# Filling a tile of partial maxima half a head early, and an eighth PSUM bank for the run-ahead maxima

## Chip, core and metric

One core of one Trainium2 chip. The metric is the device time of one execution in microseconds, the median over several runs. The engines named below are PE (TensorE, with PEld for its weight loads), DVE (VectorE), ACT (ScalarE), POOL (GpSimd) and SP (SyncE, which issues most of the DMAs). Each engine works through its own queue in order, and waits on semaphores for the others.

## What is computed

Two full multi-head attentions over the same input, mixed by a gate of each token. x has 2048 tokens of 512 features; each attention (A and B) has 32 heads of 16 features, and all is float32.

```python
def mha(x, wqkv, wo):                      # once with A's weights, once with B's
    q, k, v = split((x @ wqkv))            # 32 heads, 16 features each
    scores = einsum("bhqd,bhkd->bhqk", q, k) * 16 ** -0.5
    o = einsum("bhqk,bhkd->bhqd", softmax(scores, axis=-1), v)
    return o.reshape(1, 2048, 512) @ wo

g = sigmoid((x * gate_w).sum(-1, keepdims=True))
return g * mha(x, wqkv_a, wo_a) + (1 - g) * mha(x, wqkv_b, wo_b)
```

## The kernel before

The order of all instructions on every engine is written by hand (a manual schedule); only the semaphores come from the framework, which also rotates the buffers of each tile name. So an instruction can wait for another engine, but never moves past one ahead of it in its own queue.

**Prologue.** x and the weights are split into a high part and a low rest, and q, k and v are projected from these (`project_qk`, L237; `project_v`, L262) into PSUM tiles `ps_pro` (two tiles of two banks each). The results go to DRAM and come back in a stacked layout, `q_st` and `k_st` (three buffers each, one for each head in flight).

**Maxima ahead of the scores.** The softmax needs the maximum of each row of scores. The kernel computes the scores twice: once only for the maxima, some 20 tiles of 128 queries ahead of their use, and once for the exponentials. A tile of maxima has 2048 keys in four parts of 512. `max_part` makes one part: a PE matmul into one bank of `ps_m` (L124, three banks) and a DVE reduction (L130) to one column of `mxp[h]`, a tile of 128 x 16 x 4 for a head h. `max_excess` and `max_pair` make two parts at once, by an ACT step (L139) and a fused DVE step (L146). As a pair then leaves one of the four columns of `mxp` unwritten, the tile is filled with a very low number first (L118, on POOL). `mxp` rotates over two buffers. In `max_tile` the fill is issued when the first part of a head's first tile is, directly ahead of it in program order. When a head is complete, `max_split` reduces the four columns to one (L154, DVE), and POOL splits the result into two parts (`mparts`, L155 and L156); `max_rows` transposes them (L161, DVE) and sends them through DRAM into rows of `q_st`, from where the score matmuls subtract them.

**Run-ahead.** The first 80 parts (20 tiles) are made in the prologue: `run_ahead(n)` pops n parts, from the tenth block of `project_qk` on and between the tiles of the second attention's `project_v`, four after nearly every tile. In the prologue `ps_m` holds three banks and `ps_pro` four; one of the eight is not used. After the prologue `ps_pro`'s banks go to `ps_st` (four banks of scores) and the eighth to `acc`.

**Main loop.** 64 heads of 16 rounds; one iteration is two rounds, r and r+1, so a head has eight iterations. The order within an iteration is a string,

```python
FULL = "mree2emem3ememef3me"
```

in which e is a block of scores with its exponential (`score`: PE L614 into `ps_st`, ACT L616), m, r and f are `max_part`, `max_excess` and `max_pair` for the tile 20 rounds ahead, and a digit is that many quarters of the product of the probabilities with V (`attend_next`, PE L565, accumulated in `acc`, evicted once a head by ACT, L582). At the first digit the output projections that are due (`project_out`, L449, with their DVE steps L453 or L455) are put in, and, one iteration after the end of a head of maxima, `max_rows`. The variable m is r + 20, so the maxima are one head and four rounds ahead. Side work is due at fixed rounds through `later` and is issued at the start of an iteration: gate products (POOL, L346, L353), loads of V (POOL's queue, L177), loads of the output weights (L388 to L390), reciprocals of the denominators (L404), normalising (POOL, L422) and splitting (POOL, L427, L428). In the last iteration of a head of maxima `max_split` is issued at its end; the next iteration begins with the side work that is due, and then `max_part` of the new head, with the fill.

Of the kernel before, what the change touches and what calls it, by code (L numbers as in the profile page):

```python
# [23 lines left out]
F32 = mybir.dt.float32  # L24
# [5 lines left out]
PSUM = bass.MemoryType.PSUM  # L30
DRAM = bass.MemoryType.DRAM

P = 128
# [4 lines left out]
NT = S // P  # L38
KC = DM // P
NQ = S // 512  # L40
NG = DM // P
HG = H // NG
NH = 2 * H
# [3 lines left out]
LOWEST = -3.0e38  # L47
# [6 lines left out]
def gated_mha(ctx: ExitStack, tc: tile.TileContext, xT, x, wqkv_a, wo_a, wqkv_b, wo_b, gate_w, out):  # L54
    nc = tc.nc
    pe, act, dve, pool = nc.tensor, nc.scalar, nc.vector, nc.gpsimd
# [6 lines left out]
    ps_m = ctx.enter_context(tc.tile_pool(name="ps_m", bufs=3, space=PSUM))  # L63
# [23 lines left out]
    def load_stacks(h, halves=HALVES):  # L87
        dma = nc.sync.dma_start
        s, hh = divmod(h, H)
        g, j = divmod(hh, HG)  # L90
        q, k = q_st[h % 3], k_st[h % 3]
        qs, ks = qd[s][g], kd[s][g]

        def pairs(t, step, n):
            v = t[0, j]
            return bass.AP(tensor=v.tensor, offset=v.offset, ap=[[n, DH], [step, 2], [1, n]])

        for b in halves:
            dma(k[b:b + 32].bitcast(F32), pairs(ks, HG * DH * KS, KS))
            dma(q[b:b + 32].bitcast(F32), pairs(qs, 0, S))  # L100
            dma(k[b + 32:b + 48].bitcast(F32), ks[0, j])
            dma(q[b + 32:b + 48].bitcast(F32), qs[1, j])
# [3 lines left out]
    mxp = {}  # L106
# [3 lines left out]
        turn[0] ^= 1  # L110
        return HALVES[1 - turn[0]]

    def max_tile(m):
        h, t = divmod(m, NT)
        if t == 0 and h not in mxp:
            mxp[h] = small.tile([P, NT, NQ], F32, name="mxp")
            if h:
                pool.memset(mxp[h], LOWEST)  # L118
        return h, t

    def max_scores(ps, h, t, c):
        q, k = q_st[h % 3], k_st[h % 3]
        b = rows()
        pe.matmul(ps, q[b:b + SC, t * P:(t + 1) * P], k[b:b + SC, c * 512:(c + 1) * 512], start=True, stop=True)  # L124

    def max_part(m, part):
        h, t = max_tile(m)
        ps = ps_m.tile([P, 512], F32, name="ps_m")
        max_scores(ps, h, t, part)
        dve.tensor_reduce(mxp[h][:, t, part:part + 1], ps, op=ALU.max, axis=AX.X)  # L130

    excess = {}

    def max_excess(m):
        h, t = max_tile(m)
        ps = ps_st.tile([P, 512], F32, name="ps_st")
        max_scores(ps, h, t, NQ)
        excess[m] = work.tile([P, 512], F32, name="excess")
        act.activation(excess[m], ps, AF.Relu)  # L139

    def max_pair(m):
        h, t = divmod(m, NT)
        ps = ps_m.tile([P, 512], F32, name="ps_m")
        max_scores(ps, h, t, 1)
        e = excess.pop(m)
        dve.tensor_tensor_reduce(e, ps, e, 1.0, LOWEST, ALU.add, ALU.max, mxp[h][:, t, 1:2])  # L146
# [3 lines left out]
    def max_split(h):  # L150
        halves = mxp.pop(h)
        m = small.tile([P, NT], F32, name="mrow")
        mp = small.tile([P, 2, NT], F32R, name="mparts")
        dve.tensor_reduce(m, halves, op=ALU.max, axis=AX.X)  # L154
        pool.tensor_copy(mp[:, 0], m)  # L155
        pool.tensor_tensor(mp[:, 1], m, mp[:, 0].bitcast(F32), op=ALU.subtract)  # L156
        mparts[h] = mp

    def max_rows(h):
        mt = small.tile([P, 32], F32, name="mt")  # L160
        dve.transpose(mt, mparts.pop(h).rearrange("p i t -> p (i t)").bitcast(F32))  # L161
        q = q_st[h % 3]
        r = md[h % 3]
        nc.sync.dma_start(r.rearrange("i (t a x) -> a (i t) x", a=4, x=32), mt)
        for b in HALVES:
            nc.sync.dma_start(q[b + SC:b + SC + 2].bitcast(F32), r)
# [11 lines left out]
                       vd[s][c * 512:(c + 1) * 512, o].rearrange("(k p) f -> p k f", p=P))  # L178

    with tc.tile_pool(name="xs", bufs=1) as xs, tc.tile_pool(name="pro", bufs=2) as pro, \  # L180
            tc.tile_pool(name="ps_pro", bufs=2, space=PSUM) as ps_pro:
        xh = [xs.tile([P, KC, 512], F32R, name=f"xh{c}") for c in range(NQ)]
        xl = [xs.tile([P, KC, 512], F32R, name=f"xl{c}") for c in range(NQ)]
        wblocks = {}
# [100 lines left out]
        def run_ahead(n):  # L285
            turn[0] = 0
            for _ in range(n):
                m, part = ahead.pop(0)
                max_part(m, part)
                if (m, part) == (NT - 1, NQ - 1):  # L290
                    max_split(0)
                    pending.append(0)

        pending = []
        for i, (s, g, isk) in enumerate(blocks):
            block(split_w, i + 1)
            block(load_w, i + 3)
            if i in (2, 8):
                load_w(i // 8, 2 * DM, DM)
            if i in (4, 9):  # L300
                split_w(i // 8, 2 * DM, DM)
            project_qk(s, g, isk, lambda: run_ahead((i >= 10) + 2 * (i >= 13)))
            if i in (5, 6, 8, 9):
                load_stacks(i // 8, HALVES[(i - 5) % 3:][:1])
            if i == 7:
                for t in range(NT):
                    project_v(0, t)
            if i == 9:
                for c in range(4):
                    load_v(0, c)  # L310
# [129 lines left out]
    def project_out(side, t):  # L440
        groups = SIDES[side]
        ps = result_bank()
        c, tt = divmod(t, 4)
        sl = slice(tt * P, (tt + 1) * P)
        for G in groups:
            n, g = gh[G] * DH, G % NG
            slot = c if G == LAST else g
            for i, (a, b) in enumerate(((0, 0), (1, 0), (0, 1))):
                pe.matmul(ps, ot[a][:n, slot, sl], wt[b][:n, g], start=G == groups[0] and i == 0,  # L449
                          stop=G == groups[-1] and i == 2)  # L450
        g = gate[min(side, 1)][:, t:t + 1]
        if side == 0:
            dve.tensor_scalar(o_acc[:, t], ps, g, None, op0=ALU.mult)  # L453
        else:
            dve.scalar_tensor_tensor(o_acc[:, t], ps, g, o_acc[:, t], op0=ALU.mult, op1=ALU.add)  # L455
# [132 lines left out]
    def attend_next(n):  # L588
        while n:
            r, qa = divmod(done[0], 4)  # L590
            qb = min(4, qa + n)
            attend(r, qa, qb)
            done[0] += qb - qa
            n -= qb - qa
# [11 lines left out]
    def score(r, c):  # L606
        h, kt = divmod(r, NT)
        if c == 0:
            pt[r] = ppool.tile([P, S], F32, name="p")
        q, k = q_st[h % 3], k_st[h % 3]  # L610
        kk, cc = (4 * (kt % 4) + c, kt // 4) if h == NH - 1 else (kt, c)
        b = rows()
        ps = score_bank(r)
        pe.matmul(ps, k[b:b + SC + 2, kk * P:(kk + 1) * P], q[b:b + SC + 2, cc * 512:(cc + 1) * 512],  # L614
                  start=True, stop=True)
        act.activation(pt[r][:, c * 512:(c + 1) * 512], ps, AF.Exp, scale=SCALE)  # L616
# [7 lines left out]
    for r in range(0, ROUNDS, 2):  # L624
        h, kt = divmod(r, NT)
        projects = []
        for rr in (r, r + 1):
            for fn, a in later.pop(rr, ()):
                if fn is project_out:
                    projects.append(a)  # L630
                else:
                    fn(*a)
        if kt == 0 and h + 2 < NH:
            load_stacks(h + 2)
        m = r + NT + LEAD
        scored, parts = 0, 2
        for step in FULL if m < ROUNDS else ():
            if step == "e":
                score(r + scored // 4, scored % 4)
                scored += 1  # L640
            elif step == "r":
                max_excess(m)
            elif step == "f":
                max_pair(m)
            elif step == "m":
                max_part(m + parts // NQ, parts % NQ)
                parts += 1
            else:
                for a in projects:
                    project_out(*a)  # L650
                projects = []
                turn[0] = 0
                if r:
                    attend_next(int(step))
                if scored > 1 and r in after:
                    max_rows(after.pop(r))
        m += 1
        if m > ROUNDS:
            for rr in (r, r + 1):
                for c in range(4):  # L660
                    score(rr, c)
                attend_next(4 * rr - done[0])
                if r in after:
                    max_rows(after.pop(r))
        if m < ROUNDS and m % NT == NT - 1:
            max_split(m // NT)
            after[r + 2] = m // NT
# [29 lines left out]
```

## Time and profile before

| | |
|---|---|
| time, median of 3 runs | 2902.99 us (2901.59 to 2903.16) |
| the profiled execution's own time | 2899.51 us |
| its span, first to last instruction | 2897.7 us |
| busy share of the span | PE 98%, ACT 84%, DVE 83%, POOL 10% |
| mean granted TensorE clock | 0.992 of full speed |
| fills of the tile of maxima (L118) | 63, some 0.15 us each |

In the lines of the profile shown below, a row of the timeline has its start and duration in microseconds, then engine, line, operation, output <- input, the shapes and a count; in brackets stands the idle time of the engine before it and whose event ended it. A row of the waits has the waiting engine, tile and line, what released it, the total, the number and the longest. A row of a window has its bounds, its length, the busy time of PE, PEld, DVE, ACT and POOL with the number of instructions, the granted clock, the busy share of the DMA engines and GB/s. A row of the chain by line gives the share of the span that the chain which ended last spent there. A wait for several semaphores is put down to the one that came last by the profile.

### The profile page before, as it was taken

The page shows a single profiled execution, that of the slowest core. Times are in us where ns is not written, and L with a number is a line of the kernel's source. Part 1 is how long each engine was busy: PE and PEld are TensorE (multiplying, and loading weights), DVE is VectorE, ACT ScalarE, POOL GpSimd, SP SyncE. Part 2 cuts the span into 40 slices and gives each one's busy share as a digit, 9 for nine tenths or more (in the row PEclk, how much of TensorE's full clock was granted, in tenths as well). Part 3 has the DMA queues.
Part 4 walks back from the last instruction along what each step waited for, and adds up shares of the span by engine and source line. Part 5 has one row for each costly group of instructions (what it writes and reads, how often), then busy time and mean ns, then how long its engine had stood idle before and what let it go on. Part 6 is the DMA issues. An engine that isn't in the chain of part 4 may idle for free.

```text
span 2897.7 us, 65030 instructions
## 1 busy us (share of the span) xinstructions
PE 2851.4 (98%) x26016; PEld 1437.6 (50%) x26016; DVE 2396.4 (83%) x4395; ACT 2420.3 (84%) x4755; POOL 280.0 (10%) x472
## 2 busy tenths in 40 slices
PE   8999999999999999999999999999999999999999
PEld 7876444444444444444444455544444444445554
DVE  3135788999999999999899878899999999988784
ACT  3221689999999999999999868899999999988785
POOL 2120133000000000000100132000000000011201
PEclk9999999999999999999999999999999999999999
DMA  7683334333322333333422433322333343324212
GB/s 260 195 255 122 79 70 92 63 60 60 70 53 51 52 66 67 59 61 59 82 53 53 109 79 83 56 55 51 64 58 60 60 78 70 59 60 98 64 22 90
DMA packets 86085, 231.61 MB, mean 80 GB/s; under 512 B 22134, under 2 KB 32342, under 8 KB 73238
## 3 DMA queue, kind: packets, MB, share of 16 engines
q1 hardware_dynamic: 83222, 218.53, 34.2%
q0 software_dynamic: 2560, 8.91, 1.2%
q8 instruction: 205, 3.36, 0.5%
q14 instruction: 98, 0.80, 0.1%
HBM read 158.46 MB, written 68.94 MB: 78 GB/s over the span
## 4 chain that ended last, share of the span: by engine, by line
PE 83%; DVE 11%; DMA 2%; POOL 2%; issue 1%; SPq 1%; ACT 0%; POOLq 0%; ACTq 0%; DVEq 0%
PE acc L565 33%; PE ps_st L614 26%; PE ps_m L124 13%; DVE mxp L130 8%; PE ps_pro L237 5%; PE ps_pro L262 3%; PE ps_m L449 2%; DVE excess L146 1%; PE ps_st L124 1%; DMA raw<-in_xT 0%; DMA qd<-part 0%; DVE mrow L154 0%; POOL o_num L422 0%; POOL mparts L155 0%; POOL mparts L156 0%
## 5 line engine op out<-in xcount | busy, mean ns | idle before, releaser
L616 ACT ACTIVATE p<-ps_st 128x512 f32<-128x512 f32 x4061 | 2135.1, 628 | 205.1 <-PE ps_m L124 92.9
L130 DVE TENSOR_REDUCE mxp<-ps_m 128x1 f32<-128x512 f32 x3092 | 1984.6, 684 | 251.6 <-PE ps_m L124 97.6
L614 PE MATMUL ps_st<-q_st,k_st 50*128 50x512 f32 x4061 | 1377.5, 442 | 0.3 <-ACT excess L139 0.3
L124 PE MATMUL ps_m<-k_st,q_st 48*128 48x512 f32 x3594 | 1304.2, 448 | 30.1 <-DVE mxp L130 24.5
L565 PE MATMUL acc<-p,vg 128*17 128x256 f32 (+2 forms) x16208 | 1195.4, 388 | 2.6 <-DVE ev L573 1.6
L614 PEld LDWEIGHTS ps_st<-q_st,k_st 50*128 50x128 f32 x4061 | 677.2, 185 | 380.9 <-ACT p L616 219.8
L124 PEld LDWEIGHTS ps_m<-k_st,q_st 48*128 48x128 f32 x3594 | 611.7, 185 | 441.4 <-DVE mxp L130 402.0
L565 PEld LDWEIGHTS acc<-p,vg 128*17 128x17 f32 x16208 | 323.6, 96 | 536.8 <-issue 412.8
L146 DVE CUSTOM_DVE_ANT_0 excess<-ps_m,excess 128x512 f32<-128x512 f32 x502 | 341.7, 681 | 0.0
L139 ACT ACTIVATE excess<-ps_st 128x512 f32<-128x512 f32 x502 | 300.9, 599 | 1.9 <-POOL k_st L81 1.8
L155 POOL CAST mparts<-mrow 128x16 fp32r<-128x16 f32 x64 | 12.6, 196 | 2095.3 <-DVE mrow L154 2095.3
L124 PE MATMUL ps_st<-k_st,q_st 48*128 48x512 f32 x502 | 206.3, 411 | 0.0
L241 ACT CAST part<-ps_pro 128x1024 fp32r<-128x1024 f32 x32 | 32.4, 1014 | 132.7 <-PE ps_pro L237 103.7
L242 DVE TENSOR_TENSOR part<-ps_pro,part 128x1024 fp32r<-128x1024 f32 x32 | 39.2, 1224 | 110.9 <-ACT part L241 91.9
L265 ACT COPY v_st<-ps_pro 128x512 f32<-128x512 f32 x31 | 18.2, 587 | 92.7 <-PE ps_pro L262 87.5
L124 PEld LDWEIGHTS ps_st<-k_st,q_st 48*128 48x128 f32 x502 | 92.9, 185 | 0.2 <-issue 0.2
L449 PE MATMUL ps_m<-wo,ot 128*128 128x512 f32 (+1 forms) x354 | 90.8, 401 | 0.0
L237 PE MATMUL ps_pro<-xh,whi 128*128 128x512 f32 x256 | 73.0, 405 | 8.6 <-ACT xh L211 8.1
L449 PEld LDWEIGHTS ps_m<-wo,ot 128*128 128x128 f32 (+1 forms) x354 | 64.0, 188 | 21.9 <-DVE mxp L146 7.5
L237 PE MATMUL ps_pro<-xh,wlo 128*128 128x512 f32 x256 | 69.4, 393 | 0.0
L237 PE MATMUL ps_pro<-xl,whi 128*128 128x512 f32 x256 | 69.3, 393 | 0.0
L237 PEld LDWEIGHTS ps_pro<-xh,whi 128*128 128x128 f32 x256 | 47.9, 191 | 23.6 <-ACT xh L211 10.2
(102 smaller groups left out, 875.6 us busy)
## 6 DMA issues: line engine op xcount, KB each, us to landing
k_st<-kd SPq DMA_DIRECT2D x128, 320.0 KB
q_st<-qd SPq DMA_DIRECT2D x128, 256.0 KB
k_st<-kd SPq DMA_DIRECT2D x128, 160.0 KB
qd<-part SPq DMA_DIRECT2D x32, 512.0 KB
kd<-part SPq DMA_DIRECT2D x32, 512.0 KB
q_st<-qd SPq DMA_DIRECT2D x128, 128.0 KB
od<-ev SPq DMA_DIRECT2D x63, 256.0 KB
vd<-v_st SPq DMA_DIRECT2D x32, 272.0 KB
```

Of the source, the lines that this page charges most:

```text
L124: pe.matmul(ps, q[b:b + SC, t * P:(t + 1) * P], k[b:b + SC, c * 512:(c + 1) * 512], start=True, stop=True)
L130: dve.tensor_reduce(mxp[h][:, t, part:part + 1], ps, op=ALU.max, axis=AX.X)
L139: act.activation(excess[m], ps, AF.Relu)
L146: dve.tensor_tensor_reduce(e, ps, e, 1.0, LOWEST, ALU.add, ALU.max, mxp[h][:, t, 1:2])
L237: pe.matmul(ps[:, c * 512:(c + 1) * 512], a[:, k], b[:, k], start=n == 0, stop=n == 3 * KC - 1)
L241: act.copy(pt[0], ps)
L242: dve.tensor_tensor(pt[1], ps, pt[0].bitcast(F32), op=ALU.subtract)
L262: pe.matmul(ps[:, :DM], a[:, k, o:o + P], b[:, k], start=n == 0, stop=n == 3 * KC - 1)
L449: pe.matmul(ps, ot[a][:n, slot, sl], wt[b][:n, g], start=G == groups[0] and i == 0, stop=G == groups[-1] and i == 2)
L565: pe.matmul(acc[32 * c:32 * c + 17, qa * P:qb * P], v[:, 4 * a + c if final else kt, j], p[:, c * 512 + qa * P:c * 512 + qb * P], start=fi ...
L614: pe.matmul(ps, k[b:b + SC + 2, kk * P:(kk + 1) * P], q[b:b + SC + 2, cc * 512:(cc + 1) * 512], start=True, stop=True)
L616: act.activation(pt[r][:, c * 512:(c + 1) * 512], ps, AF.Exp, scale=SCALE)
```

## The change

The tile `mxp[h]` is no longer made and filled by the first `max_part` of its head. Those of heads 0 and 1 are made and filled at the start of the program, and that of head h+1 when the maxima of head h are half done (at the end of the iteration in which m % 16 is 8). The buffer that it takes is that of head h-1, whose `max_split` has been issued half a head before. All tiles are now filled, head 0's too. In the run-ahead the fourth part of each tile of queries goes to a PSUM tile of its own, `ps_x`, in the bank that was not used in the prologue; it is given back with `ps_pro`'s banks.

```diff
-    def max_tile(m):
-        h, t = divmod(m, NT)
-        if t == 0 and h not in mxp:
+    def new_maxima(h):
+        if h < NH:
             mxp[h] = small.tile([P, NT, NQ], F32, name="mxp")
-            if h:
-                pool.memset(mxp[h], LOWEST)
-        return h, t
+            pool.memset(mxp[h], LOWEST)
+
+    for h in range(2):
+        new_maxima(h)
...
-    def max_part(m, part):
-        h, t = max_tile(m)
-        ps = ps_m.tile([P, 512], F32, name="ps_m")
+    def max_part(m, part, pool_of=None):
+        h, t = divmod(m, NT)
+        ps = pool_of.tile([P, 512], F32, name="ps_x") if pool_of else ps_m.tile([P, 512], F32, name="ps_m")
         max_scores(ps, h, t, part)
...
     def max_excess(m):
-        h, t = max_tile(m)
+        h, t = divmod(m, NT)
...
-            tc.tile_pool(name="ps_pro", bufs=2, space=PSUM) as ps_pro:
+            tc.tile_pool(name="ps_pro", bufs=2, space=PSUM) as ps_pro, \
+            tc.tile_pool(name="ps_x", bufs=1, space=PSUM) as ps_x:
...
                 m, part = ahead.pop(0)
-                max_part(m, part)
+                max_part(m, part, ps_x if part == NQ - 1 else None)
...
                 if scored > 1 and r in after:
                     max_rows(after.pop(r))
+        if m % NT == NT // 2:
+            new_maxima(m // NT + 1)
         m += 1
```

## Prediction

> **What bounds the kernel now.** I read the span and clock first, then the page's busy line and the shares of the chain that ended last by line, then the waits by total.
>
> ```profile
> core 0: 2897.7 us, clock 0.992
> PE 2851.4 (98%) x26016; PEld 1437.6 (50%) x26016; DVE 2396.4 (83%) x4395; ACT 2420.3 (84%) x4755; POOL 280.0 (10%) x472
> PE acc L565 33%; PE ps_st L614 26%; PE ps_m L124 13%; DVE mxp L130 8%; PE ps_pro L237 5%; PE ps_pro L262 3%; PE ps_m L449 2%; DVE excess L146 1%; PE ps_st L124 1%; DMA raw<-in_xT 0%; DMA qd<-part 0%; DVE mrow L154 0%; POOL o_num L422 0%; POOL mparts L155 0%; POOL mparts L156 0%
> ```
> ```profile
> DVE mxp L130 <- POOL mxp L118: 64.2, 58, 4.9
> PE ps_m L124 <- DVE mxp L130: 24.5, 42, 3.9
> ```
>
> PE looks like the bound at 98%, but its matmuls overlap and their ends are modelled, so a PE that waits a little inside a group still looks busy. What matters is that the chain leaves PE for DVE's L130 for 8% of the span, and that the fill of the maxima tile (L118, POOL) holds DVE up 58 times, 64.2 us in all. That wait is what the change removes. Its place is the boundary between two heads, shown by the timeline around one of them:
>
> ```profile
> 771.86 0.50 PE L614 MATMUL ps_st<-q_st,k_st 50*128 50x512 f32 x1
> 774.20 0.84 PE L565 MATMUL acc<-p,vg 128*17 128x384 f32 x8
> 775.07 0.68 DVE L146 CUSTOM_DVE_ANT_0 excess<-ps_m,excess 128x512 f32<-128x512 f32 x1
> 776.40 0.22 DVE L154 TENSOR_REDUCE mrow<-mxp 128x16 f32<-128x64 f32 x1
> 776.60 0.50 PE L614 MATMUL ps_st<-q_st,k_st 50*128 50x512 f32 x1
> 776.68 0.20 POOL L155 CAST mparts<-mrow 128x16 fp32r<-128x16 f32 x1 [37.52 <-DVE mrow L154]
> 776.96 0.22 POOL L156 TENSOR_TENSOR mparts<-mrow,mparts 128x16 fp32r<-128x16 f32 x1
> 777.12 0.15 POOL L118 MEMSET mxp<- 128x64 f32 x1
> 777.30 0.69 DVE L130 TENSOR_REDUCE mxp<-ps_m 128x1 f32<-128x512 f32 x1 [0.69 <-POOL mxp L118]
> 777.91 0.20 DVE L161 STREAM_TRANSPOSE mt<-mparts 128x32 f32<-128x32 f32 x1
> 779.77 0.84 PE L565 MATMUL acc<-p,vg 128*17 128x384 f32 x8
> 780.40 0.68 DVE L146 CUSTOM_DVE_ANT_0 excess<-ps_m,excess 128x512 f32<-128x512 f32 x1
> 781.10 0.60 ACT L616 ACTIVATE p<-ps_st 128x512 f32<-128x512 f32 x1 [0.96 <-PE ps_st L614]
> ```
>
> DVE ends the old head (L154), and its first reduction of the new head waits until POOL has cast, subtracted and only then filled the new tile. The bill on PE: from the scores after the first attends to the last group of attends an undisturbed iteration takes 774.20 - 771.86 = 2.34 us, this one 779.77 - 776.60 = 3.17, so 0.83 is lost, because the three banks of ps_m come free late. ACT shows it as 0.96 us idle. ACT and DVE are nearly full in the other iterations, so none of it is made up later.
>
> **The tile filled early.** The fill is issued eight rounds ahead, in front of L155 in POOL's queue. L155 starts here after 37.52 us of idle POOL and only for want of mrow, so a fill ahead of it is long done. DVE can then begin the new head at about 776.66 instead of 777.30. The transpose L161 is next in its queue and needs L156, which ends at 777.18; one reduction (777.91 - 777.30 = 0.61) puts the transpose at 777.27. The hole is thus filled by a reduction and does not move on to L161, though only by 0.09 us. I take 0.60 of the 0.69: about 0.04 stays for the hand-over, and about 0.05 goes where PE's own order (the third matmul of the group) becomes the limit. Bounds: 0.83 (all that PE loses) and nothing (if DVE is not what PE waits for).
>
> The holes are not all alike; rows of each kind, in the timeline of DVE:
>
> ```profile
> 345.52 0.69 DVE L130 TENSOR_REDUCE mxp<-ps_m 128x1 f32<-128x512 f32 x1 [1.94 <-POOL mxp L118]
> 586.74 0.69 DVE L130 TENSOR_REDUCE mxp<-ps_m 128x1 f32<-128x512 f32 x1 [0.69 <-POOL mxp L118]
> 663.01 0.69 DVE L130 TENSOR_REDUCE mxp<-ps_m 128x1 f32<-128x512 f32 x1 [0.23 <-POOL mxp L118]
> 816.21 0.69 DVE L130 TENSOR_REDUCE mxp<-ps_m 128x1 f32<-128x512 f32 x1 [1.47 <-POOL mxp L118]
> 1427.53 0.69 DVE L130 TENSOR_REDUCE mxp<-ps_m 128x1 f32<-128x512 f32 x1 [1.52 <-PE acc L565]
> 1623.51 0.69 DVE L130 TENSOR_REDUCE mxp<-ps_m 128x1 f32<-128x512 f32 x1 [3.14 <-POOL mxp L118]
> 2594.83 0.69 DVE L130 TENSOR_REDUCE mxp<-ps_m 128x1 f32<-128x512 f32 x1 [4.90 <-POOL mxp L118]
> 2641.27 0.69 DVE L130 TENSOR_REDUCE mxp<-ps_m 128x1 f32<-128x512 f32 x1 [3.17 <-POOL mxp L118]
> 2782.73 0.69 DVE L130 TENSOR_REDUCE mxp<-ps_m 128x1 f32<-128x512 f32 x1 [0.69 <-POOL mxp L118]
> ```
>
> - 36 like the first (586.74 the first, 2782.73 the last): 36 x 0.60 = 21.6 us.
> - Eight of 0.22 to 0.32 at ends of a group of heads, where a reciprocal fills most of the hole: 8 x 0.2 = 1.6.
> - Ten of 1.47 to 1.94, where a gate product or the issue of a V load stands ahead of the fill on POOL. Four of them (1427.53 is one) name another releaser and aren't in the 64.2. None of that POOL work stands ahead of L156, so all of it goes, less the 0.09: they add up to 17.0, so 16.1.
> - Two long ones (1623.51, 2594.83) behind normalising on POOL, with no projection on PE to cover them: 3.14 + 4.90 - 0.18 = 7.9.
> - Six of 3.14 to 3.95 in heads that project out. There PE works through most of the hole, so I measure on PE as above:
>
> ```profile
> 2640.39 0.50 PE L614 MATMUL ps_st<-q_st,k_st 50*128 50x512 f32 x1
> 2644.38 0.84 PE L565 MATMUL acc<-p,vg 128*17 128x384 f32 x8
> 1669.73 0.50 PE L614 MATMUL ps_st<-q_st,k_st 50*128 50x512 f32 x1
> 1673.10 0.84 PE L565 MATMUL acc<-p,vg 128*17 128x384 f32 x8
> ```
>
> 3.99 and 3.37 instead of 2.34: 1.65 (four such) and 1.03 (two), 8.7 together; the upper bound is the holes' own 3.17. DVE's next stop there is the result of the projection (L453, L455), which PE delivers in either case.
>
> Holes together: 21.6 + 1.6 + 16.1 + 7.9 + 8.7 = 55.9 us.
>
> **The clock.** A mean clock of 0.992 is (1 - 0.992) x 2 x 2897.7 = 46.4 us at half rate. The windows show seven stretches; one is at the start of the main loop, ahead of any hole, and each of the other six begins less than 4 us after a hole over 1.4 us. One of them, and the two evictions of acc around it:
>
> ```profile
> 1430.97:1437.80 6.83, 6.83 (x44) 2.63 (x46) 4.11 (x8) 4.37 (x9) 1.87 (x2) 0.50 0.15 43
> 1401.34 0.61 ACT L582 COPY ev<-acc 128x512 f32<-128x512 f32 x1
> 1443.19 0.67 ACT L582 COPY ev<-acc 128x512 f32<-128x512 f32 x1
> ```
>
> That head takes 41.85 us; the head from 777.30 to 816.21 has a hole within 0.05 of the same size and takes 38.91. So 6.83 us at half rate cost 41.85 - 38.91 - 0.05 = 2.89 us (bounds 0 and 3.41). None of the 36 heads with a hole of 0.69 has such a stretch, so I expect none where the holes are gone: 6/7 x 46.4 = 39.8 us, x 2.89/6.83 = 16.8 us.
>
> [...]
>
> **The eighth bank.** In the second projection of V each tile of tokens is followed by four blocks of maxima, and the fourth waits for one of three banks:
>
> ```profile
> PE ps_m L124 <- DVE mxp L130: 7.2, 13, 0.6
> 270.60 0.73 PE L124 MATMUL ps_m<-k_st,q_st 48*128 48x512 f32 x3
> 272.30 1.20 PE L262 MATMUL ps_pro<-wvhi,xh 128*128 128x512 f32 x4
> 215.72 0.73 PE L124 MATMUL ps_m<-k_st,q_st 48*128 48x512 f32 x3
> 216.39 1.19 PE L237 MATMUL ps_pro<-xh,whi 128*128 128x512 f32 x4
> ```
>
> The first row is the wait between 240 and 311 us: 13 tiles, 0.55 each as PE idle. From the first block to the next projection PE needs 1.70 us; three blocks without a wait, earlier, need 0.67, and a fourth adds 0.1 to 0.23. So 0.80 to 0.93 a tile is saved; I take 0.85, 13 x 0.85 = 11.0 us (bounds 7.2 and 12.1). DVE reduces four blocks in about 2.5 us (4 x 0.61) and has about 3.8 per tile, so it doesn't become the limit. The new bank becomes free for acc at the loop's start by DVE's own order: nothing.
>
> Everything else costs nothing: two fills at the start run on an idle POOL, and the 62 others (0.15 us each) beside a POOL that is 10% busy. No DMA is added or moved, so SP's queue is as before, and POOL's V loads only come 0.15 us earlier.
>
> **Sum.** 55.9 + 16.8 + 11.0 = 83.7 us off the profiled execution's 2899.5, which gives 2815.8. The median of the runs shown is 3.5 above it: 2903.0 - 83.7 = 2819.
>
> **Rivals.**
> 1. The slow stretches stay or move. [...] Against: no head with a small hole has one. 2903.0 - 66.9 = 2836.
> 2. DVE's hole is not what PE waits for: PE or ACT, at nearly full load, takes its place. Then only PE's recorded waits go, 24.5 - 7.2 = 17.3 in the loop, with 16.8 and 11.0: 2858. Against: the third matmul of the group waits for DVE in the boundary iteration alone, and ACT stands idle there.
> 3. Slower: the fill comes late. It now stands in POOL's order behind instructions that wait for a DMA:
>
> ```profile
> POOL num L346 <- DMA num<-in_x: 96.8, 12, 16.8
> ```
>
> The longest, 16.8 us, nearly reaches from the middle of a head to its end (four iterations of some 4.6 us, 18.3). Were POOL's waits longer, DVE would stop for the rest of it. To undo the sum it would need 83.7/62 = 1.35 us more at every boundary than before; 2904 at 1.4 us, 2910 at 1.5. Against: L155 stands behind the fill and starts promptly.
> 4. The wait is not removed (the first reduction waits for something later on POOL's queue), and the bank brings half: 2897.
>
> **How the numbers follow.** Chances: forecast 0.76, rival 1 0.14, rival 2 0.05, rival 4 0.03, rival 3 0.02. The range: the bounds upward of the gain (0.69 in each small hole, 3.2 more; half of the hidden part of the six projecting heads, 5; 3.41 a stretch, 3; the bank, 1) lead to 2807, and a further 3 for what later iterations win back, 2804; the other end takes in rival 1 with 0.4 us in the small holes, 2843, and 2 for the spread of runs, 2845. A measurement of this kernel tells 0.2%, some 6 us, from no change: faster 0.95, same 0.03, slower 0.02.
>
> **What would show it.** Right: L118 is no longer a releaser of L130; L130 follows L154 within about 0.05 us and L161 comes one reduction later; an ordinary head takes 37.5 us instead of 38.1; the clock's mean is about 0.998; a tile of the second V projection takes about 3.8 us instead of 4.65 and L124 waits there for nothing. Wrong: L161 waits for L156, the hole only having moved; slow stretches at other places; PE still waiting for DVE's L130 in the boundary iteration.

## The result, and the profile after

The changed kernel takes 2810.1 us (2809.4 to 2811.7), the kernel before 2903.1; the ratio is 0.968, with a 95% interval of 0.967 to 0.970. The forecast was 2819, in a range of 2804 to 2845. The two profiled executions are 2810.6 and 2899.5, 88.9 apart where the sum said 83.7. (The kernel before varies with its clock: its runs beside the experiments took 2901.3 us at a mean clock of 0.992 and 2908.8 at 0.988.)

Span and clock, the page's busy line and the chain by line, for the kernel after. The program's lines behind the pools of the prologue (from L182 on) have moved by one: L614 is L615, L616 is L617, L565 is L566, L262 is L263; the fill L118 is L116.

```profile
core 0: 2808.8 us, clock 0.999
PE 2789.1 (99%) x26016; PEld 1429.3 (51%) x26016; DVE 2397.4 (85%) x4395; ACT 2416.8 (86%) x4755; POOL 280.2 (10%) x473
PE acc L566 38%; PE ps_st L615 31%; PE ps_m L124 14%; PE ps_pro L238 5%; PE ps_m L450 3%; PE ps_pro L263 3%; PE ps_st L124 1%; DMA qd<-part 1%; DMA raw<-in_xT 1%; DMA q_st<-qd 0%; DVE mxp L130 0%; DMA rb<-rd 0%; DMA vd<-v_st 0%; PE ps_st L450 0%; PE ps_st L501 0%
```

DVE's L130 has gone from 8% of the chain to 0%, and the clock from 0.992 to 0.999. PE's busy time fell by 62 us although it does the same matmuls. Within the span 47.8 us were at half rate before and 6.8 are after, which accounts for part of it; the rest is probably time that the profile's modelled ends of matmuls counted as busy while PE waited, but the two were not told apart. The fill no longer stands among the releasers of anything.

The timeline at an ordinary boundary after the change:

```profile
743.92 0.69 DVE L130 TENSOR_REDUCE mxp<-ps_m 128x1 f32<-128x512 f32 x1
744.64 0.22 DVE L154 TENSOR_REDUCE mrow<-mxp 128x16 f32<-128x64 f32 x1
744.77 0.68 DVE L130 TENSOR_REDUCE mxp<-ps_m 128x1 f32<-128x512 f32 x1
744.84 0.50 PE L615 MATMUL ps_st<-q_st,k_st 50*128 50x512 f32 x1
744.92 0.20 POOL L155 CAST mparts<-mrow 128x16 fp32r<-128x16 f32 x1 [36.83 <-DVE mrow L154]
745.20 0.22 POOL L156 TENSOR_TENSOR mparts<-mrow,mparts 128x16 fp32r<-128x16 f32 x1
745.46 0.21 DVE L161 STREAM_TRANSPOSE mt<-mparts 128x32 f32<-128x32 f32 x1
747.31 0.84 PE L566 MATMUL acc<-p,vg 128*17 128x384 f32 x8
748.65 0.60 ACT L617 ACTIVATE p<-ps_st 128x512 f32<-128x512 f32 x1 [0.27 <-PE ps_m L124]
```

The first reduction of the new head starts 0.13 us after L154 does, where it was 0.90 before. PE goes from the scores to the last attends in 747.31 - 744.84 = 2.47 us, where it was 3.17, and 2.34 is the undisturbed time: of the 0.83 lost, 0.13 is left. ACT's idle of 0.96 is 0.27.

The evictions of acc give the length of a head, in the kernel before (the first two rows) and after:

```profile
751.97 0.61 ACT L582 COPY ev<-acc 128x512 f32<-128x512 f32 x1
790.08 0.61 ACT L582 COPY ev<-acc 128x512 f32<-128x512 f32 x1
757.61 0.61 ACT L583 COPY ev<-acc 128x512 f32<-128x512 f32 x1
795.03 0.61 ACT L583 COPY ev<-acc 128x512 f32<-128x512 f32 x1
```

38.11 us have become 37.42.

In the prologue, the chain of the kernel after around one tile of the second projection of V, in order of time:

```profile
263.81 2.94 PE ps_pro L263 x12
266.74 0.66 PE ps_m L124 x3
267.40 0.00 PE ps_x L124
267.41 2.72 PE ps_pro L263 x11
```

The chain is PE alone. A tile takes 267.41 - 263.81 = 3.60 us instead of 4.65, and the fourth block adds nothing to the third.

### The profile page after: what moved, and what is told of

Same layout as the page of the kernel before. It is cut to its first block, busy times and chain, and to the rows that moved or that the text cites. A ratio compares the mean times of both kernels' runs of the same rounds, so it can differ in the third digit from the quotient of the medians.

```text
span 2808.8 us, 65084 instructions
## 1 busy us (share of the span) xinstructions
PE 2789.1 (99%) x26016; PEld 1429.3 (51%) x26016; DVE 2397.4 (85%) x4395; ACT 2416.8 (86%) x4755; POOL 280.2 (10%) x473
## 4 chain that ended last, share of the span: by engine, by line
PE 96%; DMA 2%; DVE 1%; SPq 1%; ACT 0%; issue 0%; POOL 0%; DVEq 0%; ACTq 0%
PE acc L566 38%; PE ps_st L615 31%; PE ps_m L124 14%; PE ps_pro L238 5%; PE ps_m L450 3%; PE ps_pro L263 3%; PE ps_st L124 1%; DMA qd<-part 1%; DMA raw<-in_xT 1%; DMA q_st<-qd 0%; DVE mxp L130 0%; DMA rb<-rd 0%; DMA vd<-v_st 0%; PE ps_st L450 0%; PE ps_st L501 0%
## 5 line engine op out<-in xcount | busy, mean ns | idle before, releaser
L617 ACT ACTIVATE p<-ps_st 128x512 f32<-128x512 f32 x4061 | 2131.0, 628 | 132.4 <-PE ps_m L124 71.4
L130 DVE TENSOR_REDUCE mxp<-ps_m 128x1 f32<-128x512 f32 x3072 | 1977.0, 684 | 150.5 <-PE ps_m L124 69.7
L615 PE MATMUL ps_st<-q_st,k_st 50*128 50x512 f32 x4061 | 1353.9, 438 | 0.3 <-ACT excess L139 0.3
L124 PE MATMUL ps_m<-k_st,q_st 48*128 48x512 f32 x3574 | 1265.4, 444 | 1.3 <-DVE mxp L130 0.7
L566 PE MATMUL acc<-p,vg 128*17 128x256 f32 (+2 forms) x16208 | 1187.5, 386 | 3.0 <-DVE ev L574 2.0
L615 PEld LDWEIGHTS ps_st<-q_st,k_st 50*128 50x128 f32 x4061 | 675.0, 184 | 379.6 <-ACT p L617 227.7
L124 PEld LDWEIGHTS ps_m<-k_st,q_st 48*128 48x128 f32 x3574 | 602.3, 184 | 365.1 <-DVE mxp L130 327.1
L566 PEld LDWEIGHTS acc<-p,vg 128*17 128x17 f32 x16208 | 322.7, 96 | 530.4 <-issue 404.4
L155 POOL CAST mparts<-mrow 128x16 fp32r<-128x16 f32 x64 | 12.6, 196 | 2038.1 <-DVE mrow L154 2038.1
L124 PE MATMUL ps_st<-k_st,q_st 48*128 48x512 f32 x502 | 205.2, 409 | 0.0
L124 PEld LDWEIGHTS ps_st<-k_st,q_st 48*128 48x128 f32 x502 | 92.1, 183 | 0.2 <-issue 0.2
```

Source lines behind the costliest of these rows:

```text
L566: pe.matmul(acc[32 * c:32 * c + 17, qa * P:qb * P], v[:, 4 * a + c if final else kt, j], p[:, c * 512 + qa * P:c * 512 + qb * P], start=fi ...
```

## The experiments

**The two parts by themselves.** The early fill with three banks for the run-ahead, and the bank with the fill at the head's first part:

```diff
 # fill alone
-                max_part(m, part, ps_x if part == NQ - 1 else None)
+                max_part(m, part)
 # bank alone: max_tile and its memset as before the change, with
+                max_part(m, part, ps_x if part == NQ - 1 else None)
```

> The early fill alone, without the extra bank. Theory (boundary holes and the half-rate stretches behind them carry the change, the bank adds only its own 13 tiles x 1.05 us): 2810.1 + 13.6 = 2824 us (2820 to 2828), clock 0.998 or more. Rival (the two parts help each other, since the bank's loop also keeps PE's clock up or DVE's start early): outside that, 2835 or more. Rival (slow stretches don't come from the holes): the clock stays at 0.993 or less.

Measured: 2824.2 us (2823.6 to 2824.4), ratio 0.972 (0.971 to 0.974), clock 0.998.

> The extra bank alone, with the fill at the head's first part as before. Theory: 2903 - 13.6 = 2889.5 us (2885 to 2894; the half-rate stretches may fall elsewhere, since all later times shift), clock about 0.992. Rival (the start of the main loop is bound by DVE or a DMA and gives the bank's gain back): 2900 or more.

Measured: 2889.5 us (2886.5 to 2890.2), ratio 0.9945 (0.993 to 0.996), clock 0.991. The gains of the two, against the 2903.1 of before, are 79 and 13.5 us and add up to the 93 of the change (against the 2904.2 that the kernel before took beside these runs they are 80 and 15, the same within 2 us). The half-rate stretches go with the fill, not with the bank.

**Is it the lead, or the place in the queue?** The fill is issued at the end of the old head's last iteration, directly ahead of `max_split`.

```diff
-        if m % NT == NT // 2:
-            new_maxima(m // NT + 1)
...
         if m < ROUNDS and m % NT == NT - 1:
+            new_maxima(m // NT + 1)
             max_split(m // NT)
```

> The fill is issued at the end of the head's last iteration, directly ahead of max_split, instead of half a head before; it stands ahead of the cast L155 on POOL's queue, but only just. Theory (what counts is that the fill doesn't stand behind the cast, the subtraction and the side work of the next round, not that it is early): 2810 us, within 3. Rival (the lead of half a head is needed, since POOL is late at the boundary): 2825 or more, and L130 waits for the fill at ten or more boundaries.

Measured: 2810.8 us (2808.5 to 2812.9), ratio 0.968 (0.966 to 0.970): as the changed kernel. Half a head of lead isn't needed; the fill must only not stand behind the cast, the subtraction and the side work of the next round.

**Is it the wait, or the fill?** The fill stays at the boundary, on DVE:

```diff
-            pool.memset(mxp[h], LOWEST)
+            (pool if h < 2 else dve).memset(mxp[h], LOWEST)
...
-        if m % NT == NT // 2:
-            new_maxima(m // NT + 1)
...
             max_split(m // NT)
+            new_maxima(m // NT + 1)
```

> The fill stays at the boundary, behind max_split, but on DVE itself, which needs no wait. Theory (it was the wait for POOL that cost, not the fill): only some 0.10 to 0.20 us of DVE work per ordinary boundary comes on top of the changed kernel, about 56 x 0.15 = 8 us: 2818 us (2812 to 2824). Rival (any step between the last reduction of a head and the first of the next costs what POOL's did, since PE's banks come free later): 2840 or more.

Measured: 2818.3 us (2817.3 to 2819.8), ratio 0.970 (0.969 to 0.972). DVE's timeline at one boundary of this kernel:

```profile
783.40 0.22 DVE L154 TENSOR_REDUCE mrow<-mxp 128x16 f32<-128x64 f32 x1
783.58 0.11 DVE L116 MEMSET mxp<- 128x64 f32 x1
783.79 0.69 DVE L130 TENSOR_REDUCE mxp<-ps_m 128x1 f32<-128x512 f32 x1
```

L130 comes 0.39 after L154 instead of 0.13, and 8 us are lost. So of the 79 us that the fill's move brings, some 71 were the wait for POOL and what followed from it.

**Do the holes slow the clock?** In the kernel before, the fill is repeated on POOL, which makes the hole at every boundary longer; of the rest only POOL's work behind the fill comes later, too.

```diff
-                pool.memset(mxp[h], LOWEST)
+                for _ in range(5):              # 3, 9, 17 in the others
+                    pool.memset(mxp[h], LOWEST)
```

> The kernel before, with the fill repeated five times on POOL at the same place, so the hole at an ordinary boundary grows from 0.69 to some 1.3 us. The holes alone: 56 x 0.6 = 34 us more, 2937. [...] Rival (stretches come by chance or from elsewhere): 2937, clock 0.991 to 0.992.

> The same with nine fills: holes of some 1.9 us at the ordinary boundaries. The holes alone: 56 x 1.2 = 67 us more, 2970. Theory (four of ten holes of 1.47 to 1.94 us had a half-rate stretch behind them): about 40% of the ordinary boundaries and most of the larger ones get one, 20 to 35 in all, each some 2.9 us: 3020 to 3060, clock 0.960 to 0.978. [...]

> The same with seventeen fills: holes of some 3.1 us, PE idle for some 2 us in each. The holes alone: 56 x 2.4 = 134 us more, 3037. Theory: a stretch behind nearly every boundary, 50 to 60, each some 3 us: 3170 to 3230, clock 0.93 to 0.95. [...]

> The kernel before with three fills: holes of some 1.1 us at the ordinary boundaries (0.21 per fill, as the runs with five, nine and seventeen showed), between 0.69 (no stretch behind 36) and 1.53 (a stretch behind most). The holes alone: 56 x 0.42 = 24 us, 2926. If the clock answers in proportion to the hole: some 15 more stretches, 2960 to 2980, clock 0.975 to 0.985. If there is an edge close to 1.4 us: 2926 to 2935, clock 0.988 to 0.992.

Measured, one run each: 2950.7, 3030.8, 3135.2 and 3272.7 us with three, five, nine and seventeen fills. Span and clock of each, then DVE's row at one ordinary boundary of each, in this order (in these kernels L118 is L119, L124 is L125 and L130 is L131):

```profile
core 0: 2948.7 us, clock 0.981
core 0: 3028.7 us, clock 0.960
core 0: 3133.2 us, clock 0.941
core 0: 3270.9 us, clock 0.920
```
```profile
1064.93 0.69 DVE L131 TENSOR_REDUCE mxp<-ps_m 128x1 f32<-128x512 f32 x1 [1.10 <-POOL mxp L119]
```
```profile
1050.74 0.69 DVE L131 TENSOR_REDUCE mxp<-ps_m 128x1 f32<-128x512 f32 x1 [1.52 <-POOL mxp L119]
```
```profile
819.81 0.69 DVE L131 TENSOR_REDUCE mxp<-ps_m 128x1 f32<-128x512 f32 x1 [2.36 <-POOL mxp L119]
```
```profile
803.67 0.69 DVE L131 TENSOR_REDUCE mxp<-ps_m 128x1 f32<-128x512 f32 x1 [4.04 <-POOL mxp L119]
```

A fill takes 0.21 us of POOL's time in such a series, not the 0.15 of its row, so the holes were larger than the first three expectations assumed. Within the span, the trace's record of the clock has 17, 39, 57 and 63 half-rate stretches, 114, 242, 369 and 526 us in all, against 7 and 48 in the kernel before and 1 and 7 in the changed one. The time follows: with five fills the holes alone are 56 x 0.84 = 47 us, and 194 us more at half rate at 2.89 per 6.83 are 82, together 129, which with the 2902 measured beside it gives 3031. With three, 24 + 28 give 2957 (2951 measured, the kernel before beside it at 2905), with nine 94 + 136 give 3132 (3135); with seventeen the same sum gives 3292, 19 too many, and why is open. None of the four times is one that was given before it: those with five, nine and seventeen fills are above every time named for them, and the one with three fills falls between its two ranges. The rival that stretches come by chance would have left the clock at 0.991; it is out.

Which holes the stretches follow says more than the totals. The clock's record, set beside DVE's holes, shows this: of the 36 ordinary boundaries, none has a stretch behind it at 0.69 us, none at 1.10, 19 at 1.52, 30 at 2.36 and 35 at 4.04. The ten more with three fills all come elsewhere: the 18 longer holes, now 1.9 to 5.3 us, have 14 instead of 6, and two come after the last hole. The totals look like a gradual answer, but an edge between 1.10 and 1.52 us isn't excluded by these runs; the 2926 to 2935 expected for one missed because it counted no new stretches behind the longer holes. The clock (third number from the end) in the 6.83 us from the row shown on, with three and with five fills:

```profile
1064.93:1071.76 6.83, 6.55 (x66) 2.93 (x58) 6.46 (x13) 5.57 (x12) 0.00 (x0) 1.00 0.04 10
```
```profile
1050.74:1057.57 6.83, 6.20 (x32) 2.06 (x32) 5.14 (x11) 4.41 (x9) 0.00 (x0) 0.75 0.04 10
```

PE's recorded idle at a boundary with five fills is short of a microsecond in all (0.34 + 0.19 us):

```profile
805.44 0.50 PE L125 MATMUL ps_m<-k_st,q_st 48*128 48x512 f32 x1 [0.34 <-DVE mxp L131]
806.13 0.50 PE L125 MATMUL ps_m<-k_st,q_st 48*128 48x512 f32 x1 [0.19 <-DVE mxp L131]
```

In the record of the clock the stretches last 3.41, 6.83 or 10.24 us in the kernel before, whole multiples of 3.41 (but for the last, which the end of the record cuts off); so PE's work is read here in windows of 3.41 us, counted from the starts of the stretches. Two of them in the kernel before, each right behind a hole on DVE (of 1.52 and 1.47 us), the first followed by a stretch and the second not (length, then PE's busy time):

```profile
1427.55:1430.97 3.42, 2.78 (x16) 0.96 (x18) 3.42 (x7) 2.20 (x4) 0.00 (x0) 1.00 0.35 93
816.58:819.99 3.41, 2.84 (x18) 1.18 (x19) 3.41 (x9) 1.91 (x4) 0.00 (x0) 1.00 0.34 91
```

PE is busy for 81% of the first and 83% of the second. In the kernel before and those with three and five fills all 60 windows ahead of a stretch lie at 83% or less, leaving out the one stretch of each at the start of the main loop (86 to 89% before it). But 23 other windows at full rate are as low and have no stretch behind them, 8 of them in the kernel before (15 of the 23 lie in heads that project out or after the last hole). So a low share is not enough, and what starts a stretch was not shown; the shares are read from modelled ends of matmuls.

**What the boundary still costs.** Two variants of the changed kernel: `max_rows`, with the transpose L161, at the second digit of the iteration, and, beside that, `max_split` at the first digit of the next iteration instead of the end of the last.

```diff
 # rows later
-                if scored > 1 and r in after:
+                if scored > 2 and r in after:
 # split later, too
-            max_split(m // NT)
             after[r + 2] = m // NT
...
+                if scored == 2 and r in after:
+                    max_split(after[r])
```

> The changed kernel with the transpose L161 (and its DMAs) issued at the second digit of the iteration instead of the first, some 1.4 us later. Theory (what a boundary still costs, 0.28 us per ordinary head, is DVE's extra work ahead of the reductions that free PE's banks): the transpose's 0.13 us and its 0.08 us wait for POOL leave that place: 0.1 to 0.2 us x 56 less, 2799 to 2805 us. Rival (PE alone is the bound now): 2810, within 2.

Measured: 2805.3 us (2805.1 to 2806.2), ratio 0.967 (0.965 to 0.968), at the upper end of what was expected.

> As the one with the transpose later, and max_split (the reduction L154, the cast and the subtraction) issued at the first digit of the next iteration, two reductions later. Theory (as above): nearly all of the 0.28 us per ordinary head goes, since DVE has idle time later in the iteration: 2794 to 2801 us. Rival (PE alone is the bound): 2810, within 2. Rival (the maxima reach q_st too late for the scores of that head): 2815 or more, with PE or PEld L615 waiting for the DMA of q_st.

Measured: 2802.6 us (2801.5 to 2806.8), ratio 0.966 (0.965 to 0.967): the fastest. Two evictions of acc in the last one:

```profile
717.37 0.62 ACT L583 COPY ev<-acc 128x512 f32<-128x512 f32 x1
754.65 0.61 ACT L583 COPY ev<-acc 128x512 f32<-128x512 f32 x1
```

The head takes 37.28 us instead of 37.42, and in the variant with the transpose alone most heads take the same 37.28. So the transpose ahead of the reductions was the 0.13 us that PE still lost, 56 x 0.13 = 7.3 us, and the place of L154 costs nothing. The second variant meets this at 2810.1 - 7.3 = 2802.8; the first has 7 us more at half rate in its profile (13.7 against 6.8 in the span), about 3 us. The expectation for the second, 2794 to 2801, missed by 1.6: it took all 0.28 us of the boundary iteration as DVE's; half of it is not, and what it is was not tried. No wait for q_st's DMA appeared.

## Why the prediction was right, step by step

The step on which all rested, that the fill on POOL's queue held DVE and DVE held PE's banks, is shown from four sides: alone it brings 79 of 93 us, its place in the queue decides and not its lead, the same fill without the wait costs a tenth, and a longer wait costs more. The sum against the two profiles, from the differences of the evictions of acc:

| term | predicted | measured |
|---|---|---|
| 36 ordinary boundaries | 21.6 | 23.7 |
| eight short holes | 1.6 | 3.2 |
| six of 1.47 to 1.92 with no stretch behind | 9.1 | 9.8 |
| six projecting heads | 8.7 | 9.0 |
| six holes with a stretch: holes 14.8, clock 16.8 | 31.6 | 31.3 |
| run-ahead and its bank | 11.0 | 13.6 |
| DMAs of the prologue | 0 | -1.3 |
| after the last eviction | 0 | -0.4 |
| sum (the terms are rounded) | 83.7 | 88.9 |

- The ordinary boundary was mis-sized, 0.60 for 0.70 us. The hand-over was taken as 0.04 after the end of L154; the two reductions overlap, and L130 starts while L154's row still runs (it starts at 744.77, and L154 ends at 744.86). The margin of 0.09 us for the transpose was used up: L156 ends at 745.42 and L161 starts at 745.46, 0.69 instead of 0.61 after the reduction. That is the 0.08 us by which one of the signs of being wrong, L161 waiting for L156, did come.
- The eight short holes brought 0.39 us each, twice the 0.2 of the sum. In seven of them L130 now comes 0.60 us after L154, with the reciprocal between them, where it came 0.91 after it; so 0.31 is from there, more than the hole's 0.23, since the rows overlap. The rest was not followed.
- Two of the 36 brought 0.00 and 0.02 us instead of 0.60. In them PE projects out at the boundary, and DVE's next step waits for that, before (the first row) and after the change alike:

```profile
1820.16 0.75 DVE L453 TENSOR_SCALAR o_acc<-ps_m,gate 128x512 f32<-128x512 f32 x1 [1.15 <-PE ps_m L449]
1758.81 0.63 PE L566 MATMUL acc<-p,vg 128*17 128x256 f32 x8
1758.92 0.75 DVE L454 TENSOR_SCALAR o_acc<-ps_m,gate 128x512 f32<-128x512 f32 x1 [1.90 <-PE ps_m L450]
```

  In the one shown, DVE's idle of 0.69 in front of L130 has only moved: in front of the projection's result there is 1.90 - 1.15 = 0.75 more. The other projecting heads were measured on PE and came out right (1.0 to 1.1 and 1.7 to 1.8); these two were put with the ordinary ones by the size of their hole, which doesn't tell what else covers it.
- The bank was mis-sized, 0.85 for 1.05 us a tile: the fourth block was given 0.1 to 0.23 us of PE, but it runs beside the third and adds nothing, as the chain shows. Ahead of it 1.3 us were lost, in DMAs that the change does not touch. The first load of x lands 1.1 us later, as shown below, of which 0.5 is left when the second has landed; the rest comes with two later transfers on the chain (v_st to DRAM, and the parts of q):

```profile
3.68 7.67 DMA raw<-in_xT
```
```profile
3.68 8.76 DMA raw<-in_xT
```

  (the chain of before, then of after; a single execution each, so no more is made of it).
- The clock's price held together with the holes' (31.3 for 31.6; the two can't be told apart in these heads), and again in the runs with three, five and nine fills. Rival 1 fell: of 47.8 us at half rate 6.8 are left. In the kernel before, PE's waits for L130 are 0.58 us in the mean (24.5 us in 42); the longest, of 3.87, stands ahead of the longest stretch (10.24 us, from 2594.91), while in the 3.41 us ahead of each of the other five PE was idle for 0.6 to 2.2 us. The row behind the wait of 3.87:

```profile
2595.57 0.79 PE L124 MATMUL ps_m<-k_st,q_st 48*128 48x512 f32 x1 [3.87 <-DVE mxp L130]
```

  Rival 2 fell: neither PE nor ACT took DVE's place at the boundary, where PE now needs 2.47 us instead of 3.17 and ACT is idle for 0.27 instead of 0.96. Rival 3 and rival 4 did not occur: L155 starts as promptly as before, and L116 releases nothing. (Rival 3's two times are a little low: 1.4 and 1.5 us at 62 boundaries on top of 2819 give 2906 and 2912.)
- Of the 9 us between 2819 and 2810, the terms above are 5. The other 4 are no error of the sum: the profiled execution of the kernel before was 3.5 us faster than the median of its runs, that of the changed kernel 0.5 slower. The misses of the sum mostly go one way, so it did not come out by errors that cancel, but for the ordinary boundaries, where two that brought nothing make up for a part of what the other 34 brought more.
- Of what was to be seen, a head of 37.5 us was 37.4, a tile of 3.8 us 3.60, and the clock 0.999.

## What to carry to other kernels

A small step on a side engine can hold the main one through the order of its queue, as the fill of 0.15 us on POOL did here (DVE idle for 0.69 us and 0.83 lost on PE at an ordinary boundary): look at what stands ahead of it there, and move it in front of the chain that it should not follow; how far in front did not matter here (2810.8 us just ahead of it, 2810.1 half a head ahead). Price such a wait on the engine that sets the time, between two of its own rows, and add the half-rate clock that a hole can bring with it: here holes of up to 1.10 us at the 36 ordinary boundaries brought none, and 19 of the 36 of 1.52 us did (about 0.4 us for each microsecond of a stretch). Look at what else covers a hole before counting it.

## What was not expected of the hardware

PE's clock fell to half rate behind a hole although PE's recorded idle in the 3.41 us ahead of the stretch was only 0.6 us, with PE busy for 81% of them (1427.55 to 1430.97 in the kernel before). Lengthening the ordinary holes from 0.69 to 1.10 us brought no stretch behind any of the 36, and 1.52 us brought one behind 19; with the longer holes, which grew too, the stretches went from 7 to 39 and by the sum above cost more through the clock (82 us) than by themselves (47 us). A fill of 128 x 64 on POOL has a row of 0.15 us, but each further one in a series lengthens the hole by 0.21.
